# Two chunk pairs per batch, PSUM copies on one engine, and earlier sums in a fused attention and feed-forward kernel

## The chip, the cores and the metric

One Trainium2 chip, one core of it. The metric is the device time of one execution in microseconds (us). The kernel before takes 854.52 us, the median of 3 runs (854.33 to 857.35).

## The reference

Eight batches b, each with 8 heads, 512 tokens and 32 state vectors of width 64, all in float32. Attention runs in both directions between tokens and state; the results, 544 rows of 512 per batch, pass through a feed-forward block with d_ff = 2048.

```python
a     = softmax(x @ state.T / 8)        # per head, 512 x 32
xread = a @ state                       # 512 x 64 per head
a2    = softmax(state @ x.T / 8)        # per head, 32 x 512
sread = a2 @ x                          # 32 x 64 per head
t     = concat(xread, sread)            # rows of 8*64 = 512
h     = t @ w_in                        # 512 -> 2048
out   = (h * sigmoid(1.702 * h)) @ w_out    # 2048 -> 512
```

The weights arrive as 64-bit floats and are rounded to float32 on the chip.

## The kernel before, in words

**The algebra.** The token side never forms `xread`. For each batch the product of the state with `w_in` is made first, as M (128 rows of head and state by 2048 columns, held as two groups g of four heads), in four chunks c of 512 columns: `att_M(b, c)`, L336 to L343. Then `up_x(b, f)` (L408) makes one block of 128 hidden columns as a product of M and the softmax `aT`, and ScalarE applies the activation (L405) into a tile g. The second product (tiles g times `w_out`) is plain for batch 0 (`down`, L422) and a Strassen-like scheme for batches 1 to 7 and for the state rows (`strassen`, L456): seven products X, Y, X, Y, Z, Y, Z, of 32 matmul instructions each half-width, in which VectorE supplies sums of g tiles (`sums_of_g`, L447) and differences of quarters of `w_out` (T1 to T4, L613 to L615).

**The order of the work** is written out by hand; each engine takes its instructions in program order. TensorE's work on the next batch's attention is put between the halves of the seven products: `strassen` pops one of 14 slots after each half (L475), and `att_slots(b)` (L371) fills them: transposes of state and x in slots 0 to 3, scores, both softmaxes and chunk 0 of M in slot 5, chunk 1 in slot 7, chunk 2 in slot 9, transposes of the second softmax (`att_eT`) in slots 10 and 11, `att_sread` in slot 12. Chunk 3 is made among the up products of its own batch (L631). Product Z starts at slot 8.

**PSUM.** Three pools: `psA` (2 banks, tag att) for everything of the attention, `psH` (2 banks, tag h) for the up products, `psO` (4 banks, tag o) for the scores and the products X, Y, Z. In `strassen` the banks of `psO` are taken in the order X, Y, scores 0, scores 1, Z, so Z takes the bank of X again, after ScalarE has stored X (L487).

**Copies out of PSUM.** `copies(b, i)` (L246) picks the engine: ScalarE for batches 0 and 1 and for odd i, VectorE for even i of later batches. It serves `att_state` (L254), `att_xT` (L264, where batch 0 counts as a later one), `att_M` (L343, one copy per group), `att_eT` (L353) and `att_sread` (L369). In slot 5 VectorE's work of both softmaxes (L284 to L332) stands ahead of its copy of chunk 0.

**The start.** Batches 0 and 1 run while the weights are loaded and rounded piece by piece (`round_to`, L220; VectorE, with ScalarE for part of the w_in pieces). `turn(b, c, ...)` (L565) makes the four up products of one chunk. The exponentials of batches 0 and 1 (`att_s_exp`, L584 to L586) stand ahead of chunk 3 of batch 0 (L588), and so ahead of its copies on ScalarE. After the loop over f (L595 to L608), which does batch 0's second product and batch 1's last eight up products, VectorE makes T1 to T4 and the sums of batch 1 (L613 to L617), and then batch 1's products begin.

Of the kernel before, what the change touches and what calls it, by code (L numbers as in the profile page):

```python
# [10 lines left out]
FP32 = mybir.dt.float32  # L11
# [3 lines left out]
ALU = mybir.AluOpType  # L15
# [5 lines left out]
def kernel(  # L21
# [31 lines left out]
    nc = tc.nc  # L53

    B, H, S, D = x.shape
# [3 lines left out]
    P = 128  # L59
    NPR = P // Ns  # L60
    NG = H // NPR
    NF = DF // P
    SCH = S // P
    ST = S + Ns
    FC = 512
    NFC = DF // FC
    NB = S // Ns
    HF, HN = NF // 2, DM // 2
# [9 lines left out]
    konst = ctx.enter_context(tc.tile_pool(name="konst", bufs=1))  # L78
    xpool = ctx.enter_context(tc.tile_pool(name="xpool", bufs=1))
    apool = ctx.enter_context(tc.tile_pool(name="apool", bufs=1))  # L80
    mpool = ctx.enter_context(tc.tile_pool(name="mpool", bufs=3))
    gpool = ctx.enter_context(tc.tile_pool(name="gpool", bufs=1))
    opool = ctx.enter_context(tc.tile_pool(name="opool", bufs=2))
    psA = ctx.enter_context(tc.tile_pool(name="psA", bufs=2, space=bass.MemoryType.PSUM))
    psH = ctx.enter_context(tc.tile_pool(name="psH", bufs=2, space=bass.MemoryType.PSUM))
# [4 lines left out]
    def att_ps(shape, name):  # L90
        return psA.tile(shape, FP32, tag="att", name=name)
# [9 lines left out]
    T1, T2, T4 = (sums[:, i].rearrange("p (f n) -> p f n", f=HF) for i in range(3))  # L101
# [16 lines left out]
    def load_state(b):  # L118
        stn[b] = apool.tile([P, NG, D], FP32, tag="stn", name=f"stn_{b}", bufs=2)
        for g in range(NG):  # L120
            nc.sync.dma_start(stn[b][:, g], st_v[b, g])
# [15 lines left out]
    w_out = konst.tile([P, NF, DM], FP32, name="w_out")  # L137
# [29 lines left out]
    for i, v in enumerate((8.0 * most, 8.0 * (most - least))):  # L167
        t = konst.tile([P, 1], FP32, name=f"edge_{i}")
# [72 lines left out]
    srT = konst.tile([P, NPR, B, Ns], FP32, name="srT")  # L241


    A = {b: {} for b in range(B)}

    def copies(b, i):  # L246

        return nc.scalar.copy if b in (0, 1) or i % 2 else nc.vector.tensor_copy

    def att_state(b):  # L250
        ps = att_ps([P, P], f"stT_{b}")
        nc.tensor.transpose(ps, stn[b].rearrange("p g d -> p (g d)"), ident)
        A[b]["stT"] = apool.tile([P, P], FP32, tag="stT", name=f"stT_{b}", bufs=2)
        copies(b, 0)(A[b]["stT"], ps)  # L254

    def att_xT(b, j, warm=0):
        if j == 0:
            A[b]["xT"] = apool.tile([P, NPR, S], FP32, tag="xT", name=f"xT_{b}")
        ps = att_ps([P, SCH, P], f"xT_{b}_{j}")
        for c in range(SCH):  # L260
            if warm:
                keep_warm(warm)
            nc.tensor.transpose(ps[:, c], x_heads(b, c, j), ident)  # L263
        copies(b or None, j)(A[b]["xT"][:, j], ps.rearrange("p c q -> p (c q)"))  # L264

    def by_state(b, ps, rhs):

# [26 lines left out]

    def att_s_exp(b, room=None):
        a = A[b]
        a["e2"] = []
        for g in range(NG):
            e = apool.tile([P, S], FP32, tag="e2", name=f"e2_{b}_{g}", bufs=2) if room is None else room[:, g]
            sm = apool.tile([P, 1], FP32, tag="sm2", name=f"sm2_{b}_{g}", bufs=4)  # L300
            nc.scalar.activation(out=e, in_=a["s"][g], func=AF.Exp, bias=a["mx2"][g], scale=scale, accum_out=sm)  # L301
            a["e2"].append((e, sm))

    def att_s_norm(b):

        for e, sm in A[b]["e2"]:
            nc.vector.tensor_scalar(sm, sm, eps, None, ALU.add)
            nc.vector.reciprocal(out=sm, in_=sm)
            nc.vector.tensor_scalar(e, e, sm, None, ALU.mult)
# [23 lines left out]
            a["aT"].rearrange("p g t -> p (g t)"), a["e1"].rearrange("p g i n -> p (g i n)")  # L333
        )

    def att_M(b, c):  # L336

        m = mpool.tile([P, NG, FC], FP32, tag="M", name=f"M_{b}_{c}")
        A[b]["M", c] = m
        ps = [att_ps([P, FC], f"M_{b}_{c}_{g}") for g in range(NG)]  # L340
        by_state(b, ps, lambda rows, j: w_in[c][rows, j])
        for g in range(NG):
            copies(b, g)(m[:, g], ps[g])  # L343

    def att_eT(b, g):

        a = A[b]
        if g == 0:
            a["eT"] = apool.tile([P, NG, SCH, P], FP32, tag="eT", name=f"eT_{b}")
        ps = att_ps([P, SCH, P], f"eT_{b}_{g}")  # L350
        for c in range(SCH):
            nc.tensor.transpose(ps[:, c], a["e2"][g][0][:, P * c : P * (c + 1)], ident)
        copies(b, g)(a["eT"][:, g], ps)  # L353

    def att_sread(b):
        a = A[b]
        ps = att_ps([P, NPR, NG, Ns], f"sr_{b}")
        for j in range(NPR):
            for c in range(SCH):
                nc.tensor.matmul(  # L360
                    ps[:, j],
                    x_heads(b, c, j),
                    a["eT"][:, :, c, Ns * j : Ns * (j + 1)],
                    start=(c == 0),
                    stop=(c == SCH - 1),
                )
        for g in range(NG):
            r = slice(D * g, D * (g + 1))
            copies(b, g)(srT[r, :, b, :], ps[r, :, g, :])  # L369

    def att_slots(b):  # L371

        slots = [[] for _ in range(14)]

        def at(i, fn, *args):
            slots[i].append((fn, args))

        at(0, att_state, b)
        for j in range(NPR):
            at(j, att_xT, b, j)  # L380
        at(5, att_scores, b)
        at(5, att_blocks, b)
        at(5, att_s_max, b)
        at(5, att_s_exp, b)
        at(5, att_x_exp, b)
        at(5, att_s_norm, b)
        at(5, att_x_norm, b)
        at(5, att_M, b, 0)
        at(7, att_M, b, 1)
        at(9, att_M, b, 2)  # L390
        for g in range(NG):
            at(10 + g, att_eT, b, g)
        at(12, att_sread, b)
        return slots
# [13 lines left out]
    def up_x(b, f, spare=False):  # L408
        c, o = divmod(P * f, FC)
        m = A[b]["M", c]  # L410
        up(b, f, S, [m[:, g, o : o + P] for g in range(NG)], [A[b]["aT"][:, g] for g in range(NG)], spare)
# [35 lines left out]
    def sums_of_g(key, f, ntok):  # L447

        half = ntok // 2
        (a11, a21), (_, a22) = quarters(key, f, ntok), quarters(key, HF + f, ntok)  # L450
        s1, s2 = S1[:, f, :half], S2[:, f, :half]
        nc.vector.tensor_tensor(out=s1, in0=a21, in1=a22, op=ALU.add)  # L452
        nc.vector.tensor_tensor(out=a21, in0=a11, in1=a21, op=ALU.subtract)  # L453
        nc.vector.tensor_tensor(out=s2, in0=s1, in1=a11, op=ALU.subtract)
# [64 lines left out]
    nper = FC // P  # L519

    def rounds(n):
        round_to(done["b"] + n)
# [42 lines left out]
    def turn(b, c, then, n=()):  # L565

        for i in range(nper):
            if i == nper - 1 and then:
                att_M(*then)
            up_x(b, nper * c + i)  # L570
            if i < len(n):
                rounds(n[i])
# [8 lines left out]
    att_s_max(0)  # L581
    att_s_max(1)
    turn(0, 2, None, [1, 1, 1])
    room = apool.tile([P, NPR, S], FP32, tag="xT", name="e2_0")  # L584
    att_s_exp(0, room)
    att_s_exp(1)  # L586
    round_to(4 * NPR)
    att_M(0, 3)  # L588
    att_s_norm(0)
    att_s_norm(1)  # L590
    turn(0, 3, None, [1, 1])


    rest = list(range(2 * nper, NF))
    for f in range(NF):  # L595
        rounds(1)
        round_to(NFC * NPR + f + 1)
        for r in range(SCH):
            down(0, r, [f], out_x[0, r], r == SCH - 1)
        if f in (0, nper * 2):  # L600
            att_M(1, 2 + f // (nper * 2))
        if f in (0, 2):
            for g in range(NG):
                att_eT(f // 2, g)
        if f in (1, 3):
            att_sread(f // 2)
        if f % 2 == 1:
            up_x(1, rest.pop(0))  # L608
    load_state(2)
    load_x(2)  # L610


    B11, B12, B21, B22 = (w_out[:, HF * i : HF * (i + 1), HN * k : HN * (k + 1)] for i in range(2) for k in range(2))  # L613
    for t, x0, x1 in ((T1, B12, B11), (T2, B22, T1), (T4, B21, T2), (B12, B22, B12)):
        nc.vector.tensor_tensor(out=t, in0=x0, in1=x1, op=ALU.subtract)  # L615
    for f in range(HF):
        sums_of_g(1, f, S)  # L617

    nb = P // Ns
    for b in range(1, B):  # L620
        ahead = b + 1 < B
        if not ahead:
            for f in range(NF):
                up_s(f)
                if f >= HF:
                    sums_of_g("sr", f - HF, B * Ns)
            strassen("sr", B * Ns, lambda r, n: out_s[nb * r : nb * (r + 1), :, n])
        if b > 1:
            for f in range(NF):
                if f == nper + 1:  # L630
                    att_M(b, NFC - 1)  # L631
                up_x(b, f)
                if f >= HF:
                    sums_of_g(b, f - HF, S)
        strassen(b, S, lambda r, n: out_x[b, r][:, n], att_slots(b + 1) if ahead else None)
        if b + 2 < B:
            load_state(b + 2)
            load_x(b + 2)
# [30 lines left out]
```

## Time and profile before

| what | value |
|---|---|
| median of 3 runs | 854.52 us |
| the profiled execution: its own time | 855.66 us |
| the profiled execution: span | 853.9 us |
| mean granted TensorE clock | 0.971 of full speed |
| busy: PE, VectorE, ScalarE | 809.6, 344.5, 195.5 us |

The span runs from the first to the last instruction; the own time is 1.8 us more and holds what lies around the span. Engines in the rows: PE is TensorE's matmul, PEld its weight load, DVE is VectorE, ACT ScalarE, POOL GpSimd, SP the engine that issues loads. An idle time in brackets is that of the engine just before the instruction, with what ended it. PEclk is the share of full speed that the clock gate granted; the two levels are 1.0 (2.4 GHz) and 0.5 (1.2 GHz). A row of windows has its start and end, its length, the busy time of PE, PEld, DVE, ACT and POOL with the count of instructions, PEclk, the share of DMA and GB/s. One float32 matmul of the program is two MATMUL instructions in the counts.

### The profile page before, as it was taken

The page shows a single profiled execution, that of the slowest core. Times are in us where ns is not written, and L with a number is a line of the kernel's source. Part 1 is how long each engine was busy: PE and PEld are TensorE (multiplying, and loading weights), DVE is VectorE, ACT ScalarE, POOL GpSimd, SP SyncE. Part 2 cuts the span into 40 slices and gives each one's busy share as a digit, 9 for nine tenths or more (in the row PEclk, how much of TensorE's full clock was granted, in tenths as well). Part 3 has the DMA queues.
Part 4 walks back from the last instruction along what each step waited for, and adds up shares of the span by engine and source line. Part 5 has one row for each costly group of instructions (what it writes and reads, how often), then busy time and mean ns, then how long its engine had stood idle before and what let it go on. Part 6 is the DMA issues. An engine that isn't in the chain of part 4 may idle for free.

```text
span 853.9 us, 8775 instructions
## 1 busy us (share of the span) xinstructions
PE 809.6 (95%) x3620; PEld 536.8 (63%) x3620; DVE 344.5 (40%) x723; ACT 195.5 (23%) x340; POOL 35.9 (4%) x72
## 2 busy tenths in 40 slices
PE   8987999979899989998999989998999989999996
PEld 3332464458674858476765858485856859884785
DVE  4995997163504171235304161327104340211320
ACT  3676311012023021312022021312032201203100
POOL 0000000010110001000000001000100011000001
PEclk9999899989999999999899999998999999999998
DMA  9620343010030002100030003000030000000001
GB/s 254 244 97 2 124 149 80 1 49 1 25 78 0 1 13 53 37 1 13 13 77 1 1 13 89 1 1 13 25 62 1 1 25 26 1 15 10 1 13 37
DMA packets 43623, 35.17 MB, mean 41 GB/s; under 512 B 37312, under 2 KB 37312, under 8 KB 43584
## 3 DMA queue, kind: packets, MB, share of 16 engines
q1 hardware_dynamic: 37920, 25.17, 10.7%
q0 software_dynamic: 3584, 8.92, 3.2%
q10 hardware_dynamic: 2080, 0.52, 0.3%
q8 instruction: 28, 0.46, 0.2%
q14 instruction: 11, 0.09, 0.0%
HBM read 25.69 MB, written 8.91 MB: 41 GB/s over the span
## 4 chain that ended last, share of the span: by engine, by line
issue 69%; PE 19%; DVE 5%; POOL 4%; ACT 2%; DMA 1%; SPq 0%; POOLq 0%; DVEq 0%
PE h L403 7%; PE o L428 6%; POOL out_dram L490 4%; PE z L471 1%; PE y L471 1%; PE M L271 1%; PE sr L360 1%; PE x L471 1%; DMA xn<-in_x_dram 1%; PE xT L263 0%; DVE g L453 0%; ACT M L343 0%; PE s L271 0%; ACT e L301 0%; DVE w_in L199 0%
## 5 line engine op out<-in xcount | busy, mean ns | idle before, releaser
L403 PE MATMUL h<-aT,M 128*128 128x512 f32 x512 | 229.5, 604 | 9.3 <-ACT M L343 9.3
L403 PEld LDWEIGHTS h<-aT,M 128*128 128x128 f32 x512 | 97.6, 193 | 135.6 <-issue 112.4
L405 ACT ACTIVATE g<-h 128x512 f32<-128x512 f32 x120 | 71.5, 597 | 181.4 <-PE h L403 181.4
L471 PE MATMUL x<-w_out,g 128*128 128x256 f32 x448 | 100.0, 379 | 0.0
L471 PEld LDWEIGHTS x<-w_out,g 128*128 128x128 f32 x448 | 84.2, 190 | 13.9 <-issue 3.4
L271 PE MATMUL M<-w_in,stT 64*32 64x512 f32 x512 | 47.0, 659 | 17.8 <-DVE M L343 17.4
L452 DVE TENSOR_TENSOR later<-g,g 128x256 f32<-128x256 f32 (+1 forms) x64 | 26.1, 408 | 84.1 <-ACT g L405 84.1
L471 PEld LDWEIGHTS z<-sums,later 128*128 128x128 f32 x224 | 47.5, 215 | 16.7 <-issue 9.1
L471 PE MATMUL z<-sums,later 128*128 128x256 f32 x224 | 57.7, 422 | 0.0
L343 DVE COPY M<-M 128x512 f32<-128x512 f32 x24 | 16.3, 681 | 98.4 <-PE M L271 98.4
L490 POOL DMA_DIRECT2D out_dram<-osb x56 | 30.0, 541 | 588.9 <-ACT osb L487 375.3
L471 PE MATMUL y<-sums,later 128*128 128x256 f32 x224 | 52.4, 389 | 0.0
L471 PE MATMUL y<-sums,g 128*128 128x256 f32 x224 | 51.1, 382 | 0.0
L471 PE MATMUL z<-w_out,g 128*128 128x256 f32 x224 | 50.8, 381 | 0.0
L471 PE MATMUL y<-w_out,g 128*128 128x256 f32 x224 | 50.1, 382 | 0.0
L471 PEld LDWEIGHTS y<-w_out,g 128*128 128x128 f32 x224 | 42.1, 190 | 10.5 <-issue 5.0
L471 PEld LDWEIGHTS y<-sums,g 128*128 128x128 f32 x224 | 41.6, 190 | 10.2 <-issue 5.0
L471 PEld LDWEIGHTS y<-sums,later 128*128 128x128 f32 x224 | 43.1, 197 | 5.7
L343 ACT COPY M<-M 128x512 f32<-128x512 f32 x40 | 22.5, 584 | 104.6 <-PE M L271 104.6
L471 PEld LDWEIGHTS z<-w_out,g 128*128 128x128 f32 x224 | 41.6, 190 | 5.2
L271 PEld LDWEIGHTS M<-w_in,stT 64*32 64x32 f32 x512 | 7.8, 108 | 42.3 <-DVE M L343 22.8
L264 ACT COPY xT<-xT 128x512 f32<-128x512 f32 x18 | 10.6, 587 | 95.9 <-PE xT L263 95.9
(109 smaller groups left out, 763.2 us busy)
## 6 DMA issues: line engine op xcount, KB each, us to landing
later<-in_moe_w_out_dram SPq DMA_DIRECT2D x16, 512.0 KB
out_dram<-osb POOLq DMA_DIRECT2D x56, 128.0 KB, 2.0
xn<-in_x_dram SPq DMA_DIRECT2D x26, 256.0 KB
w_out<-in_moe_w_in_dram SPq DMA_DIRECT2D x12, 512.0 KB
later<-in_moe_w_in_dram SPq DMA_DIRECT2D x4, 512.0 KB
sums<-in_x_dram SPq DMA_DIRECT2D x4, 256.0 KB
out_dram<-osb POOLq DMA_DIRECT2D x4, 256.0 KB, 2.4
stn<-in_state_dram SPq DMA_DIRECT2D x16, 32.0 KB
```

The costliest lines, as they stand in the source:

```text
L264: copies(b or None, j)(A[b]["xT"][:, j], ps.rearrange("p c q -> p (c q)"))
L271: nc.tensor.matmul(ps[g][st], A[b]["stT"][rows, st], rhs(rows, j), start=True, stop=True)
L343: copies(b, g)(m[:, g], ps[g])
L360: nc.tensor.matmul(ps[:, j], x_heads(b, c, j), a["eT"][:, :, c, Ns * j : Ns * (j + 1)], start=(c == 0), stop=(c == SCH - 1),)
L403: nc.tensor.matmul(hps, lhs[i], rhs[i], start=(i == 0), stop=(i == n - 1))
L405: nc.scalar.activation(out=gt[:, :ntok], in_=hps, func=AF.Gelu_apprx_sigmoid)
L428: nc.tensor.matmul(ops, G[key, f][:, P * r : P * (r + 1)], w_out[:, f], start=(f == 0), stop=(f == NF - 1))
L452: nc.vector.tensor_tensor(out=s1, in0=a21, in1=a22, op=ALU.add)
L471: nc.tensor.matmul(ps[:, r], lhs[f][:, P * r : P * (r + 1)], rhs[:, f], start=(first and r == 0 and f == 0), stop=(f == HF - 1), skip_grou ...
L490: nc.gpsimd.dma_start(dst(nb * i + r, slice(HN * k, HN * (k + 1))), o[:, r])
```

## The change

`mpool` has four buffers for M instead of three; the room comes from the tag `e2`, whose two tiles are dropped: the exponentials of the second softmax go to the `xT` tile's room (for batches 0 and 1 both into one tile of that tag). `copies` goes: every copy out of PSUM that it served is on ScalarE, except the even xT copies of batch 0. In `att_slots`, chunks 0 and 1 of M stand in slot 5 right behind the scores and ahead of both softmaxes, and chunks 2 and 3 in slot 8; chunks 1 and 3 take banks of `psH` (argument `spare`). No chunk is made among the up products any more. At the start, chunk 3 of batch 0 stands ahead of the exponentials, a rounding piece ahead of the normalisations, and its last two up products take banks of `psA`. T1, the first seven sums of batch 1 and T2 are put into the loop of batch 0's second product, at f = 14; the last sum, T4 and the fourth difference follow the loop.

```diff
--- before.py
+++ after.py
@@ -78,7 +78,7 @@
     konst = ctx.enter_context(tc.tile_pool(name="konst", bufs=1))
     xpool = ctx.enter_context(tc.tile_pool(name="xpool", bufs=1))
     apool = ctx.enter_context(tc.tile_pool(name="apool", bufs=1))
-    mpool = ctx.enter_context(tc.tile_pool(name="mpool", bufs=3))
+    mpool = ctx.enter_context(tc.tile_pool(name="mpool", bufs=4))
     gpool = ctx.enter_context(tc.tile_pool(name="gpool", bufs=1))
     opool = ctx.enter_context(tc.tile_pool(name="opool", bufs=2))
     psA = ctx.enter_context(tc.tile_pool(name="psA", bufs=2, space=bass.MemoryType.PSUM))
@@ -243,15 +243,11 @@
 
     A = {b: {} for b in range(B)}
 
-    def copies(b, i):
-
-        return nc.scalar.copy if b in (0, 1) or i % 2 else nc.vector.tensor_copy
-
     def att_state(b):
         ps = att_ps([P, P], f"stT_{b}")
         nc.tensor.transpose(ps, stn[b].rearrange("p g d -> p (g d)"), ident)
         A[b]["stT"] = apool.tile([P, P], FP32, tag="stT", name=f"stT_{b}", bufs=2)
-        copies(b, 0)(A[b]["stT"], ps)
+        nc.scalar.copy(A[b]["stT"], ps)
 
     def att_xT(b, j, warm=0):
         if j == 0:
@@ -261,7 +257,7 @@
             if warm:
                 keep_warm(warm)
             nc.tensor.transpose(ps[:, c], x_heads(b, c, j), ident)
-        copies(b or None, j)(A[b]["xT"][:, j], ps.rearrange("p c q -> p (c q)"))
+        (nc.vector.tensor_copy if b == 0 and j % 2 == 0 else nc.scalar.copy)(A[b]["xT"][:, j], ps.rearrange("p c q -> p (c q)"))
 
     def by_state(b, ps, rhs):
 
@@ -294,9 +290,11 @@
 
     def att_s_exp(b, room=None):
         a = A[b]
+        if room is None:
+            room = apool.tile([P, NPR, S], FP32, tag="xT", name=f"e2_{b}")
         a["e2"] = []
         for g in range(NG):
-            e = apool.tile([P, S], FP32, tag="e2", name=f"e2_{b}_{g}", bufs=2) if room is None else room[:, g]
+            e = room[:, g]
             sm = apool.tile([P, 1], FP32, tag="sm2", name=f"sm2_{b}_{g}", bufs=4)
             nc.scalar.activation(out=e, in_=a["s"][g], func=AF.Exp, bias=a["mx2"][g], scale=scale, accum_out=sm)
             a["e2"].append((e, sm))
@@ -333,14 +331,15 @@
             a["aT"].rearrange("p g t -> p (g t)"), a["e1"].rearrange("p g i n -> p (g i n)")
         )
 
-    def att_M(b, c):
+    def att_M(b, c, spare=False):
 
         m = mpool.tile([P, NG, FC], FP32, tag="M", name=f"M_{b}_{c}")
         A[b]["M", c] = m
-        ps = [att_ps([P, FC], f"M_{b}_{c}_{g}") for g in range(NG)]
+        name = f"M_{b}_{c}_"
+        ps = [psH.tile([P, FC], FP32, tag="h", name=name + str(g)) if spare else att_ps([P, FC], name + str(g)) for g in range(NG)]
         by_state(b, ps, lambda rows, j: w_in[c][rows, j])
         for g in range(NG):
-            copies(b, g)(m[:, g], ps[g])
+            nc.scalar.copy(m[:, g], ps[g])
 
     def att_eT(b, g):
 
@@ -350,7 +349,7 @@
         ps = att_ps([P, SCH, P], f"eT_{b}_{g}")
         for c in range(SCH):
             nc.tensor.transpose(ps[:, c], a["e2"][g][0][:, P * c : P * (c + 1)], ident)
-        copies(b, g)(a["eT"][:, g], ps)
+        nc.scalar.copy(a["eT"][:, g], ps)
 
     def att_sread(b):
         a = A[b]
@@ -366,7 +365,7 @@
                 )
         for g in range(NG):
             r = slice(D * g, D * (g + 1))
-            copies(b, g)(srT[r, :, b, :], ps[r, :, g, :])
+            nc.scalar.copy(srT[r, :, b, :], ps[r, :, g, :])
 
     def att_slots(b):
 
@@ -378,16 +377,18 @@
         at(0, att_state, b)
         for j in range(NPR):
             at(j, att_xT, b, j)
+
         at(5, att_scores, b)
+        at(5, att_M, b, 0)
+        at(5, att_M, b, 1, True)
         at(5, att_blocks, b)
         at(5, att_s_max, b)
         at(5, att_s_exp, b)
         at(5, att_x_exp, b)
         at(5, att_s_norm, b)
         at(5, att_x_norm, b)
-        at(5, att_M, b, 0)
-        at(7, att_M, b, 1)
-        at(9, att_M, b, 2)
+        at(8, att_M, b, 2)
+        at(8, att_M, b, 3, True)
         for g in range(NG):
             at(10 + g, att_eT, b, g)
         at(12, att_sread, b)
@@ -581,14 +582,25 @@
     att_s_max(0)
     att_s_max(1)
     turn(0, 2, None, [1, 1, 1])
-    room = apool.tile([P, NPR, S], FP32, tag="xT", name="e2_0")
-    att_s_exp(0, room)
-    att_s_exp(1)
     round_to(4 * NPR)
     att_M(0, 3)
+    room = apool.tile([P, NPR, S], FP32, tag="xT", name="e2_01")
+    att_s_exp(0, room[:, :NG])
+    att_s_exp(1, room[:, NG:])
+    rounds(1)
     att_s_norm(0)
     att_s_norm(1)
-    turn(0, 3, None, [1, 1])
+    up_x(0, 3 * nper)
+    up_x(0, 3 * nper + 1)
+    up_x(0, 3 * nper + 2, True)
+    up_x(0, 3 * nper + 3, True)
+    rounds(1)
+
+
+    B11, B12, B21, B22 = (w_out[:, HF * i : HF * (i + 1), HN * k : HN * (k + 1)] for i in range(2) for k in range(2))
+
+    def T_of(t, x0, x1):
+        nc.vector.tensor_tensor(out=t, in0=x0, in1=x1, op=ALU.subtract)
 
 
     rest = list(range(2 * nper, NF))
@@ -606,15 +618,16 @@
             att_sread(f // 2)
         if f % 2 == 1:
             up_x(1, rest.pop(0))
+        if f == NF - 2:
+            T_of(T1, B12, B11)
+            for k in range(HF - 1):
+                sums_of_g(1, k, S)
+            T_of(T2, B22, T1)
+    sums_of_g(1, HF - 1, S)
+    T_of(T4, B21, T2)
+    T_of(B12, B22, B12)
     load_state(2)
     load_x(2)
-
-
-    B11, B12, B21, B22 = (w_out[:, HF * i : HF * (i + 1), HN * k : HN * (k + 1)] for i in range(2) for k in range(2))
-    for t, x0, x1 in ((T1, B12, B11), (T2, B22, T1), (T4, B21, T2), (B12, B22, B12)):
-        nc.vector.tensor_tensor(out=t, in0=x0, in1=x1, op=ALU.subtract)
-    for f in range(HF):
-        sums_of_g(1, f, S)
 
     nb = P // Ns
     for b in range(1, B):
@@ -627,8 +640,6 @@
             strassen("sr", B * Ns, lambda r, n: out_s[nb * r : nb * (r + 1), :, n])
         if b > 1:
             for f in range(NF):
-                if f == nper + 1:
-                    att_M(b, NFC - 1)
                 up_x(b, f)
                 if f >= HF:
                     sums_of_g(b, f - HF, S)
```

## Rows read from the trace of the kernel before

**Rows 1.** The page, part 1: busy time, share of the span and instructions.
```profile
PE 809.6 (95%) x3620; PEld 536.8 (63%) x3620; DVE 344.5 (40%) x723; ACT 195.5 (23%) x340; POOL 35.9 (4%) x72
```

**Rows 2.** Waits of TensorE: line, releaser, total us, times, longest us.
```profile
PE M L271 <- DVE M L343: 17.4, 6, 2.9
PE h L403 <- ACT M L343: 9.3, 5, 4.2
PE xT L263 <- DVE stT L254: 4.7, 1, 4.7
```

**Rows 3.** Windows, third to seventh product, batches 1 to 6: us, busy us, clock.
```profile
198.70:247.82 49.12, 46.22 (x266) 36.63 (x265) 18.77 (x38) 8.70 (x15) 3.21 (x6) 0.97 0.10 27
292.18:341.27 49.09, 46.19 (x267) 36.14 (x266) 18.78 (x38) 8.70 (x15) 3.21 (x6) 0.97 0.10 28
385.63:435.81 50.18, 47.28 (x266) 36.90 (x265) 18.76 (x38) 8.70 (x15) 3.21 (x6) 0.93 0.10 27
480.17:529.18 49.01, 46.10 (x266) 36.05 (x265) 18.77 (x38) 8.70 (x15) 3.21 (x6) 0.97 0.10 27
573.54:623.64 50.10, 47.20 (x266) 36.81 (x265) 18.77 (x38) 8.70 (x15) 3.21 (x6) 0.93 0.10 27
668.00:716.96 48.96, 46.06 (x267) 36.03 (x266) 18.77 (x38) 8.70 (x15) 3.21 (x6) 0.97 0.05 17
```

**Rows 4.** Timeline of TensorE, batch 2: start us, us, instruction, count, idle before.
```profile
299.18 1.09 PE L271 MATMUL s<-xT,stT 64*32 64x512 f32 x16
300.07 1.06 PE L271 MATMUL M<-w_in,stT 64*32 64x512 f32 x16
301.06 7.17 PE L471 MATMUL y<-w_out,g 128*128 128x256 f32 x32
308.17 1.04 PE L271 MATMUL M<-w_in,stT 64*32 64x512 f32 x2
...
313.89 8.05 PE L471 MATMUL z<-sums,later 128*128 128x256 f32 x32
321.88 1.09 PE L271 MATMUL M<-w_in,stT 64*32 64x512 f32 x16
```

**Rows 5.** Timeline of ScalarE, batch 2, same stretch.
```profile
302.55 1.28 ACT L301 ACT_TABLE_LOAD   x1 [9.58 <-DVE mx L292]
303.84 0.69 ACT L301 ACTIVATE e<-s,mx 128x512 f32<-128x512 f32 x1
...
305.68 1.06 ACT L320 ACTIVATE e<-e 128x1024 f32<-128x1024 f32 x1 [0.38 <-DVE e L319]
...
307.10 0.65 ACT L487 COPY osb<-x 128x256 f32<-128x256 f32 x2
```

**Rows 6.** Timeline of VectorE, batch 2, same stretch.
```profile
311.40 0.65 DVE L343 COPY M<-M 128x512 f32<-128x512 f32 x1
...
315.25 0.69 DVE L505 TENSOR_TENSOR later<-y,later 128x512 f32<-128x512 f32 x1
```

**Rows 7.** Timeline of ScalarE, batch 0: the two copies of one chunk.
```profile
72.67 1.07 ACT L343 COPY M<-M 128x512 f32<-128x512 f32 x2 [0.50 <-PE M L271]
```

**Rows 8.** Windows of chunks 2 and 3 of batch 0 and their up products.
```profile
71.47:80.38 8.91, 8.15 (x34) 3.14 (x33) 3.34 (x6) 4.68 (x8) 0.00 (x0) 1.00 0.00 0
80.38:95.00 14.62, 10.39 (x33) 4.24 (x33) 11.25 (x31) 8.70 (x16) 0.00 (x0) 0.77 0.20 59
```

**Rows 9.** Windows of the first two products of batch 1 and batch 2.
```profile
175.80:198.70 22.90, 18.19 (x82) 15.49 (x81) 13.46 (x30) 2.16 (x4) 1.08 (x2) 0.85 0.06 23
276.50:292.18 15.68, 15.68 (x82) 13.82 (x81) 3.37 (x9) 1.67 (x3) 0.00 (x0) 1.00 0.00 1
```

**Rows 10.** Timeline of VectorE before and in batch 1's first products.
```profile
174.34 2.29 DVE L615 TENSOR_TENSOR sums<-w_out,sums 128x2048 f32<-128x2048 f32 x1 [14.93 <-PE o L428]
...
187.79 0.28 DVE L254 COPY stT<-stT 128x128 f32<-128x128 f32 x1
```

**Rows 11.** Timeline of ScalarE at the end of batch 0's second product.
```profile
176.51 0.60 ACT L405 ACTIVATE g<-h 128x512 f32<-128x512 f32 x1
```

## The prediction, made before the changed kernel was run

> **What bounds the kernel now.** I read the page's first part, then TensorE's waits, then the windows of one stage across batches, then the timelines of three engines in one batch. TensorE is busy 95% of the span [rows 1], so no other engine bounds the kernel as a whole; what can be won are its pauses and what follows them. The waits name three [rows 2]: chunks of M (L271) that wait for a VectorE copy, six times 2.9 us; up products (L403) that wait for ScalarE copies, the longest 4.2 us; one transpose that waits 4.7 us for a VectorE copy of the state. These 31.4 us aren't all of the loss: the windows show a granted clock of 0.97 or 0.93 in the six stretches with the 2.9 us pause [rows 3], 0.77 around the 4.2 us one [rows 8], 0.85 around the 4.7 us one [rows 9], against 1.00 in the neighbouring windows without a pause [rows 8, 9]. So each is priced as a window with its pause against the same work without it.
>
> **Slots of six batches.** In slot 5 VectorE has both softmaxes ahead of its copy of chunk 0, made by TensorE at 301.1; the copy begins at 311.40 [rows 4, 6]. Chunk 1 needs that bank: two of its sixteen instructions run at 308.17, the rest only after the copy, so product Z begins at 313.89 and ends at 321.88, slowed [rows 4]. The same work without the pause, from the same batch [rows 3, 4]: third product 7.00 (292.18 to 299.18), scores 0.89, chunk 0 0.99, the fourth product 7.11, chunk 1 another 0.99, Z the 7.00 of the third product, and the rest 19.39 (321.88 to the window's end at 341.27): 43.37. The six windows sum to 296.46; 6 x 43.37 = 260.22; so 36.2 us are lost. The change removes the cause, since no copy of M stands behind VectorE's softmaxes, and chunk 1 takes other banks than chunk 0.
>
> What it adds on the path is ScalarE's order in slot 5: four copies ahead of the exponentials, and behind them the store of X, whose bank Z needs. Worked out on batch 2: chunk 0 ends at 301.1, and two copies take 1.07 [rows 7]; chunk 1 ends at 302.1, and its copies run to 303.4. VectorE's part of the row maximum is done by then (the table load began at 302.55 [rows 5]). Table load 1.3, two exponentials 1.4 (0.69 each [rows 5]): 306.1. The wide exponential, whose input was ready by 305.68 [rows 5], 1.0: 307.1; store 0.65: 307.8, against 307.75 (307.10 + 0.65) before [rows 5]. The copy of M that stood between them is gone, so ScalarE hands the bank back at about the same time. TensorE reaches Z at 301.06 + 0.99 + 7.11 = 309.2 [rows 4]. The slack is 1.4 us, and I cost the edit at nothing; without that cover, every further us of delay costs six.
>
> Four copies in a row and M in up-product banks don't occur in the trace; their bounds are nothing (the slack holds) and, as if all four copies were exposed, 2.14 a batch, 12.8 us. I take nothing, as the nearest row (the wide exponential's start) sets the same time as before. VectorE's order gets shorter by a copy before the fourth product's sum (L505, at 315.25 [rows 6]) and its normalisation starts about 0.6 later; the second reading of Y waits for that sum only after Z and two chunks, at 309.2 + 7.0 + 2.0 = 318.2, so 3 us of cover.
>
> On two engines the copies of a chunk end after 0.65 [rows 6], on one after 1.07 [rows 7]: 0.42 more per chunk. Nobody waits: behind chunks 0 and 1 stands the fourth product, behind 2 and 3 the second half of Z, with banks of their own. The Trainium skill (PSUM — Partial Sum Buffer, in the part Engine access) has ScalarE and VectorE reading PSUM in parallel at full bandwidth as long as no bank collides, which speaks against giving all to one. By it, four chunks in six batches would lose 10 us, and the sum below would be 39 us instead of 49; no wait in the rows here collects them.
>
> Chunk 3 moves from the up products to slot 8: 1 us, moved, not saved. The state, xT, eT and read-out copies that go to ScalarE find it idle between slots (8.70 us busy in 49 [rows 3]): nothing. Four buffers for M, with the exponentials in xT's room, cost nothing: the scores have read xT before the exponentials, and the next xT comes after the eT transposes.
>
> **The start.** The four up products behind chunk 2 take 8.91 with the chunk; those behind chunk 3, the same work, 14.62 [rows 8], because chunk 3's copies stand behind four exponentials and a table load. With the copies first it should be 8.91 again: 5.7 us. What is late next are the activations behind the exponentials: copies to 82.6 (80.38 + 1.09 + 0.1 + 1.07), load 1.3, four exponentials 2.7, load 1.3: 87.9, the last activation at about 90.3. The products don't wait, having two banks of psH and two of psA; the first to need one is chunk 2 of batch 1, one f of `down` after 89.3.
>
> **The sums.** Batch 1's first two products take 22.90, batch 2's 15.68 [rows 9]: 7.2 us. In between VectorE worked from 174.34 to 187.79 on two differences and eight sums ahead of the copy of the state [rows 10]. Before 174.34 it had been idle 14.9 us [rows 10], and that idle time is the cover for seven sums and T2 (13.45 covers two differences at 2.29 and eight sums: 1.1 each, 7.8 for seven). The last sum waits for the activation ending at 177.1 [rows 11], then 1.1: 178.2. The second product would start 7.8 after the first, half of 15.68 [rows 9], at 183.6; its needs, T2 and the sums, are met 5 us earlier. T4 and the last difference end at 182.8 and are needed later still. The state's copy is on ScalarE. The loads moved behind the sums in the code are alone on SP's queue in the same order, and POOL's stores change by tenths: nothing.
>
> **The sum.** 36.2 + 5.7 + 7.2 = 49.1 us off the profiled execution's 855.66 us (span 853.9 and 1.8 around it) gives 806.5. The median of the runs is 1.1 below that execution: 805.4.
>
> **The rivals.**
> *Clock.* The pauses go, but the clock falls all the same: scores and two chunks now make 3 us of small-tile matmuls, where 2 us stood together. For it: every drop in these six windows comes beside chunks. Against: scores and chunk 0, 2 us of it, are followed by 7.11 for the fourth product against 7.00, no drop, in the same batch [rows 4]; the drops come with the pause. Price: what the windows lost beyond the pause, (36.2 - 17.4) / 6 = 3.1 us each, 19 for six: 824; half of that 815.
> *A one-off gain fails.* The up products of chunk 3 wait for activations after all (811.1) or the second product for T2 and the sums (812.6). Against: covers of 3 and 5 us above.
> *A new wait at Z.* ScalarE returns X's bank late by 1 to 4 us after using up the slack. With the wait come six times that, and some clock: 811 to 830. Against: 1.4 us of slack, from durations that all have rows.
> *Slower.* The same place with another price: Z held so long that it eats everything. That takes 49.1 / 6 = 8.2 us a batch, so X's store at 318.8 instead of 307.8, later than VectorE's whole chain in the slot (315.25 [rows 6]); at 10 us a batch it is 805.4 + 60 = 865. Only if the store waited for the normalisations and more would this happen, and ScalarE's order has no such wait.
> *It doesn't do what it says.* A copy of M in slot 5 could still be held by VectorE through another engine order; then the six windows stay, and only the start and the sums gain: 841.6. The program order leaves no room for that.
>
> **How the numbers follow.** Forecast 805.4, chance 63%; clock 14%; a one-off gain failing 13%; a short wait at Z 7%; as before in the slots 1%; slower 2%. Below, the range goes to 801: the chunks side by side may save a tenth at each change of tile shape, and the runs spread by 3 us. Above, to 818, it takes in the one-off cases, half the clock case and the lower end of the wait at Z, and the 12.8 us bound of the copies. A measurement of this kernel tells about 0.5%, 4 us. Faster by more: 0.97; within: 0.01; slower: 0.02.
>
> **What would show it.** Right: no wait of L271 for L343 of 2.9 us; the six windows at 44.4 (43.37 and chunk 3) with a clock of 1.00; chunk 3's window at 8.9; batch 1's first two products at 15.7; TensorE without idle time before Z. Wrong: idle time before Z, put down to the store of X; a clock below 1.00 behind slot 5 or 8 without a pause; up products waiting for L405 behind the exponentials; VectorE still at sums when the second product of batch 1 is due.

## The result, and the profile after

The changed kernel takes 804.82 us (median of 4 runs, 802.3 to 805.03) against 854.67 us in the same comparison: a ratio of 0.9404, 95% interval 0.9377 to 0.943. The forecast was 805.4 us. The profiled execution is the shortest of the four, 802.30 us with a span of 800.5; the other three have spans of 803.0 to 803.3 at a mean clock of 0.995 instead of 0.997. So a part read from its trace is compared with the same part of the trace before, and times only with medians.

The page's head and first part after the change, and TensorE's two largest waits, of eight (line, releaser, total us, times, longest us):

```profile
span 800.5 us, 8798 instructions
...
PE 782.1 (98%) x3618; PEld 530.4 (66%) x3620; DVE 314.4 (39%) x669; ACT 219.4 (27%) x394; POOL 36.1 (5%) x72
```

```profile
PE h L404 <- ACT M L342: 5.8, 5, 2.1
PE warm L113 <- DVE one L107: 1.2, 1, 1.2
...
```

Two of the three waits of [rows 2] are gone: no chunk of M (now L267) waits for a copy, no transpose for the state's copy (the six waits not shown are of 1.0 us or less). The up products' wait for M's copies (now L404 for L342) falls from 9.3 to 5.8, its longest piece from 4.2 to 2.1. TensorE is busy 98% of the span instead of 95% [rows 1].

The windows that answer to [rows 3], [rows 8] and [rows 9] (start:end, length, busy time of PE, PEld, DVE, ACT, POOL with counts, granted clock, DMA share, GB/s), the last row being the 16 up products of batch 2:

```profile
79.85:88.67 8.82, 8.07 (x34) 3.33 (x34) 6.53 (x21) 8.15 (x16) 0.00 (x0) 1.00 0.18 61
169.47:185.15 15.68, 15.68 (x83) 13.83 (x82) 5.76 (x6) 3.60 (x7) 1.08 (x2) 1.00 0.09 33
185.15:229.14 43.99, 43.99 (x282) 35.87 (x281) 16.05 (x33) 11.88 (x22) 3.23 (x6) 1.00 0.11 30
272.28:316.28 44.00, 44.00 (x283) 35.88 (x281) 16.12 (x33) 11.88 (x22) 3.22 (x6) 1.00 0.11 31
359.42:403.42 44.00, 44.00 (x283) 35.88 (x281) 16.11 (x33) 11.88 (x22) 3.23 (x6) 1.00 0.11 30
446.56:490.56 44.00, 44.00 (x283) 35.88 (x282) 16.13 (x33) 11.88 (x22) 3.22 (x6) 1.00 0.11 31
533.70:577.70 44.00, 44.00 (x283) 35.88 (x282) 16.12 (x33) 11.88 (x22) 3.22 (x6) 1.00 0.11 30
620.84:664.84 44.00, 44.00 (x283) 35.88 (x282) 16.11 (x33) 11.88 (x22) 3.23 (x6) 1.00 0.06 19
...
229.14:256.61 27.47, 27.47 (x66) 12.16 (x65) 8.72 (x23) 8.96 (x15) 1.07 (x2) 1.00 0.16 32
```

The stretch from the third to the seventh product takes 44.00 us, the same in all six batches to 0.01, at a clock of 1.00; before it took 48.96 to 50.18 at 0.93 or 0.97 [rows 3], with one chunk less in it. Chunk 3 of batch 0 takes 8.82 us with its up products, as forecast from chunk 2 (8.91 [rows 8]). Batch 1's first two products take 15.68 us, exactly what batch 2's took before [rows 9].

The up products of a batch, now without a chunk between them, took this long before:

```profile
247.82:276.50 28.68, 28.68 (x81) 12.26 (x80) 9.42 (x24) 9.54 (x16) 1.07 (x2) 1.00 0.14 31
```

TensorE and ScalarE in the slots of batch 2 (start us, us, instruction, count, idle before), as in [rows 4] and [rows 5]:

```profile
279.29 1.09 PE L267 MATMUL s<-xT,stT 64*32 64x512 f32 x16
280.17 1.92 PE L267 MATMUL M<-w_in,stT 64*32 64x512 f32 x32
282.02 7.17 PE L472 MATMUL y<-w_out,g 128*128 128x256 f32 x32
289.03 3.62 PE L472 MATMUL z<-sums,later 128*128 128x256 f32 x16
292.58 1.95 PE L267 MATMUL M<-w_in,stT 64*32 64x512 f32 x32
```

```profile
281.38 2.05 ACT L342 COPY M<-M 128x512 f32<-128x512 f32 x4 [8.31 <-PE M L267]
...
284.75 0.69 ACT L299 ACTIVATE e<-s,mx 128x512 f32<-128x512 f32 x1
285.33 0.19 ACT L299 ACTIVATION_READ_ACCUMULATOR e<-s,mx 128x1 f32 x1
...
287.03 0.64 ACT L488 COPY osb<-x 128x256 f32<-128x256 f32 x2
```

Scores and two chunks run in 2.7 us, then the fourth product at once, and Z at 289.03 without a wait. On ScalarE the four copies take 2.05 us, the exponentials follow, and the store of X ends at 287.67, 1.36 us ahead of Z.

### The profile page after: what moved, and what is told of

It is laid out like the page before. It is cut to its first block, busy times and chain, and to the rows that moved or that the text cites. A ratio compares the mean times of both kernels' runs of the same rounds, so it can differ in the third digit from the quotient of the medians.

```text
span 800.5 us, 8798 instructions
## 1 busy us (share of the span) xinstructions
PE 782.1 (98%) x3618; PEld 530.4 (66%) x3620; DVE 314.4 (39%) x669; ACT 219.4 (27%) x394; POOL 36.1 (5%) x72
## 3 DMA queue, kind: packets, MB, share of 16 engines
HBM read 25.69 MB, written 8.91 MB: 43 GB/s over the span
## 4 chain that ended last, share of the span: by engine, by line
issue 69%; PE 22%; POOL 4%; DVE 2%; ACT 1%; DMA 1%; SPq 0%; POOLq 0%
PE h L404 7%; PE o L429 7%; POOL out_dram L491 4%; PE y L472 2%; PE x L472 2%; PE M L267 1%; PE z L472 1%; PE sr L359 1%; DMA xn<-in_x_dram 1%; PE xT L259 0%; ACT M L342 0%; PE s L267 0%; DVE w_in L199 0%; DVE w_in L198 0%; DVE later L197 0%
## 5 line engine op out<-in xcount | busy, mean ns | idle before, releaser
L404 PE MATMUL h<-aT,M 128*128 128x512 f32 x512 | 223.9, 594 | 5.8 <-ACT M L342 5.8
L404 PEld LDWEIGHTS h<-aT,M 128*128 128x128 f32 x512 | 96.5, 190 | 127.5 <-issue 113.6
L342 ACT COPY M<-M 128x512 f32<-128x512 f32 x64 | 33.2, 595 | 96.9 <-PE M L267 96.9
L472 PE MATMUL z<-sums,later 128*128 128x256 f32 x224 | 51.1, 382 | 0.0
L472 PE MATMUL y<-sums,later 128*128 128x256 f32 x224 | 50.5, 379 | 0.0
L472 PEld LDWEIGHTS z<-sums,later 128*128 128x128 f32 x224 | 42.1, 190 | 10.5 <-issue 5.0
L490 DVE TENSOR_TENSOR osb<-z,later 128x256 f32<-128x256 f32 x28 | 10.6, 420 | 92.3 <-PE z L472 92.3
L499 DVE TENSOR_TENSOR later<-y,later 128x512 f32<-128x512 f32 x7 | 4.8, 692 | 87.8 <-PE y L472 87.8
L260 ACT COPY xT<-xT 128x512 f32<-128x512 f32 x30 | 17.6, 587 | 63.4 <-PE xT L259 63.4
L267 PE MATMUL M<-w_in,stT 64*32 64x512 f32 x512 | 33.7, 594 | 0.4 <-DVE w_in L199 0.4
```

The costliest lines, as they stand in the source:

```text
L260: (nc.vector.tensor_copy if b == 0 and j % 2 == 0 else nc.scalar.copy)(A[b]["xT"][:, j], ps.rearrange("p c q -> p (c q)"))
L267: nc.tensor.matmul(ps[g][st], A[b]["stT"][rows, st], rhs(rows, j), start=True, stop=True)
L342: nc.scalar.copy(m[:, g], ps[g])
L404: nc.tensor.matmul(hps, lhs[i], rhs[i], start=(i == 0), stop=(i == n - 1))
L472: nc.tensor.matmul(ps[:, r], lhs[f][:, P * r : P * (r + 1)], rhs[:, f], start=(first and r == 0 and f == 0), stop=(f == HF - 1), skip_grou ...
L490: nc.vector.tensor_tensor(out=o[:, r], in0=ps[:, r], in1=with_[:, r], op=ALU.add)
```

## The experiments

**Copies alone.** The kernel before, with every attention copy on ScalarE (batch 0's even xT copies stay).

```diff
-        return nc.scalar.copy if b in (0, 1) or i % 2 else nc.vector.tensor_copy
+        return nc.scalar.copy if b is not None or i % 2 else nc.vector.tensor_copy
```

> The kernel before with all its attention copies of batches 2 to 7 on ScalarE, and nothing else. Queue theory (the 2.9 us pause comes only from VectorE's softmaxes standing ahead of the copy of chunk 0): on ScalarE the copies follow the wide exponential and end at about 307.7 on batch 2's time scale, before chunk 1 is due at 308.2, so the six windows from the third to the seventh product fall from 49.4 to 43.4 us each, 36 us in all. In batch 1's first products the state's copy no longer waits, but the second product still waits for the sums (due at 183.6, ready at 187.5), so 2 to 3 of the 7.2 us come too: about 815 us. Rival (the pairs are needed, a copy beside the scores is what removes the pause): chunk 1 still waits in slot 7, windows stay near 49, about 850 us.

Measured: 814.21 us (813.34 to 814.99), ratio 0.9513 (0.9494 to 0.9533). Its windows (batch 1's first two products; batch 2 from the third product; batch 2's up products) and ScalarE's copies in batch 2:

```profile
176.53:193.53 17.00, 16.21 (x82) 13.65 (x81) 11.97 (x27) 3.60 (x7) 1.08 (x2) 1.00 0.08 31
281.39:324.89 43.50, 43.50 (x267) 35.36 (x266) 15.99 (x33) 11.01 (x20) 3.22 (x6) 1.00 0.11 31
324.89:353.57 28.68, 28.68 (x82) 12.26 (x80) 8.72 (x23) 10.03 (x17) 1.07 (x2) 1.00 0.16 30
```

```profile
294.88 1.06 ACT L320 ACTIVATE e<-e 128x1024 f32<-128x1024 f32 x1 [0.38 <-DVE e L319]
295.85 1.05 ACT L343 COPY M<-M 128x512 f32<-128x512 f32 x2
```

The copies of chunk 0 start right behind the wide exponential, at 295.85, and end before chunk 1 runs at 297.4; the window is 43.50 us at full clock, where the sum had 43.37. The pairs are not needed to end the pause: this one line takes the time from 855.82 to 814.21 us in the same comparison, most of what the whole change brings. One part was missed: the first two products take 17.00 us, so taking the copies of the state and of xT off VectorE alone gives back 5.9 of the 7.2 us, not 2 to 3.

**Pairs alone.** The kernel before with the new slots, four buffers for M and the exponentials in xT's room; the choice of engine stays.

```diff
...
+        at(5, att_M, b, 0)
+        at(5, att_M, b, 1, True)
         at(5, att_blocks, b)
...
-        at(5, att_M, b, 0)
-        at(7, att_M, b, 1)
-        at(9, att_M, b, 2)
+        at(8, att_M, b, 2)
+        at(8, att_M, b, 3, True)
...
-                if f == nper + 1:
-                    att_M(b, NFC - 1)
```

> The kernel before with chunks 0 and 1 beside the scores and chunks 2 and 3 in slot 8 (four buffers for M, exponentials in xT's room), but even copies of batches 2 to 7 still on VectorE; start and sums as before. Queue theory: VectorE's two copies now stand ahead of the softmaxes, the pause goes, the windows with four chunks take 44.0 to 44.4 us, 36 to 39 us less in all; VectorE's softmaxes start 1.3 us later, so the store of X ends at about 308.7 on batch 2's scale, still ahead of Z at 309.0. About 816 to 818 us; the 4.7 us wait for the state's copy stays. Rival (one engine for the copies is needed): Z or chunk 2 waits 1 us or more in each batch, windows 45.5 or more, 825 us or more.

Measured: 815.06 us (814.06 to 816.37), ratio 0.9528 (0.951 to 0.9545). The same windows, and the first copies in batch 2's slot 5 on VectorE and on ScalarE:

```profile
174.62:196.91 22.29, 17.58 (x82) 14.92 (x81) 13.45 (x30) 2.16 (x4) 1.08 (x2) 0.92 0.06 24
284.05:328.05 44.00, 44.00 (x283) 35.88 (x282) 19.37 (x39) 9.38 (x16) 3.22 (x6) 1.00 0.11 30
328.05:355.51 27.46, 27.46 (x65) 12.16 (x64) 8.73 (x23) 8.96 (x15) 1.07 (x2) 1.00 0.17 32
```

```profile
293.09 0.69 DVE L346 COPY M<-M 128x512 f32<-128x512 f32 x1 [8.52 <-PE M L271]
```

```profile
293.19 0.59 ACT L346 COPY M<-M 128x512 f32<-128x512 f32 x1 [8.35 <-PE M L271]
```

The two engines copy a chunk's two groups side by side, in 0.69 us. That agrees with the Trainium skill (PSUM — Partial Sum Buffer, Engine access), by which ScalarE and VectorE can access PSUM in parallel. It is worth nothing here, for TensorE waits for neither form. The window and the up products are those of the changed kernel to 0.01 us. So with the pairs the engine of the copies makes no difference in the slots; the 4.7 us wait of [rows 2] stays in the first products, 22.29 us.

**The slots undone**, copies and placement both, with the changed start and sums kept.

```diff
...
-            nc.scalar.copy(m[:, g], ps[g])
+            copies(b, g)(m[:, g], ps[g])
...
-        at(5, att_M, b, 0)
-        at(5, att_M, b, 1, True)
...
-        at(8, att_M, b, 2)
-        at(8, att_M, b, 3, True)
+        at(5, att_M, b, 0)
+        at(7, att_M, b, 1)
+        at(9, att_M, b, 2)
...
+                if f == nper + 1:
+                    att_M(b, NFC - 1)
```

> The changed kernel with the old slots and the old choice of engine for the copies; the changed start and the early sums stay. Theory of three separate gains: the six windows are back at 49 to 50 us with 2.9 us of wait each, the start and the first products of batch 1 keep their gain: 841 to 844 us. Rival (the gains overlap, for instance through the clock): outside 838 to 846 us.

Measured: 843.60 us, one run, inside the forecast. TensorE's wait and the windows (batch 1's first two products; batch 2 from the third product):

```profile
PE M L271 <- DVE M L346: 17.4, 6, 2.9
```

```profile
170.05:185.73 15.68, 15.68 (x83) 13.83 (x82) 7.25 (x9) 2.16 (x4) 1.08 (x2) 1.00 0.09 33
279.17:329.35 50.18, 47.28 (x266) 36.91 (x265) 18.77 (x38) 8.69 (x15) 3.21 (x6) 0.93 0.10 26
```

The six pauses of 2.9 us are back, and the first products keep their 15.68 us although the state's copy is on VectorE again: with the sums out of the way it has nothing to wait behind.

**The start undone.**

```diff
-    round_to(4 * NPR)
-    att_M(0, 3)
     room = apool.tile([P, NPR, S], FP32, tag="xT", name="e2_01")
     att_s_exp(0, room[:, :NG])
     att_s_exp(1, room[:, NG:])
-    rounds(1)
+    round_to(4 * NPR)
+    att_M(0, 3)
     att_s_norm(0)
     att_s_norm(1)
-    up_x(0, 3 * nper)
...
-    rounds(1)
+    turn(0, 3, None, [1, 1])
```

> The changed kernel with the start undone: the four exponentials stand ahead of chunk 3 of batch 0, normalisations ahead of both rounding pieces, the last up products in their old banks. Theory: the window of chunk 3 and its up products goes back from 8.8 to 14.6 us, with a lower clock behind the pause: 805 + 5.7 = 810.5 us. Rival (a later stage hides it): 805 us.

Measured: 808.95 us (807.55 to 810.48), ratio 0.9456 (0.9435 to 0.9476). On TensorE's timeline the 4.2 us pause is back, followed by slowed up products:

```profile
79.95 1.09 PE L267 MATMUL M<-w_in,stT 64*32 64x512 f32 x16
85.27 8.80 PE L404 MATMUL h<-aT,M 128*128 128x512 f32 x16 [4.23 <-ACT M L342]
93.91 3.60 PE L429 MATMUL o<-w_out,g 128*128 128x512 f32 x8
```

From chunk 3 to the second product it is 93.91 - 79.95 = 13.96 us instead of 8.82: 5.1 us, against 5.7 in the sum. The run undoes three edits at once (the order of chunk 3 and the exponentials, of the rounding pieces, and the banks); that the first is the one that counts rests on the releaser of the pause, the copy of M. The clock's part differs from execution to execution: the four up products ran 9.47 us behind this pause in the trace before, 8.80 here, 7.13 without it.

**The sums undone**, with the state's copy left on ScalarE.

```diff
-        if f == NF - 2:
-            T_of(T1, B12, B11)
-            for k in range(HF - 1):
-                sums_of_g(1, k, S)
-            T_of(T2, B22, T1)
-    sums_of_g(1, HF - 1, S)
+    load_state(2)
+    load_x(2)
+    T_of(T1, B12, B11)
+    T_of(T2, B22, T1)
     T_of(T4, B21, T2)
     T_of(B12, B22, B12)
-    load_state(2)
-    load_x(2)
+    for k in range(HF):
+        sums_of_g(1, k, S)
```

> The changed kernel with the four differences of w_out quarters and the eight sums of batch 1 behind the loop again; the state's copy stays on ScalarE. Theory (the sums themselves were late by 4 us, besides the copy behind them): batch 1's second product waits 3 to 4 us and then runs slowed, the window of its first two products takes 19.5 to 22 us instead of 15.7: 809 to 811 us. Rival (only the state's copy behind the sums mattered): 15.7 and 805 us.

Measured: 806.11 us (804.16 to 806.81), ratio 0.942 (0.9389 to 0.9451), not to be told from the changed kernel by time. The window of the first two products and TensorE's waits in it:

```profile
172.44:189.43 16.99, 16.21 (x82) 13.66 (x81) 11.97 (x27) 3.61 (x7) 1.08 (x2) 1.00 0.08 31
```

```profile
180.33 2.76 PE L472 MATMUL y<-sums,later 128*128 128x256 f32 x12
183.44 0.70 PE L472 MATMUL y<-sums,later 128*128 128x256 f32 x2 [0.35 <-DVE later L455]
184.57 0.70 PE L472 MATMUL y<-sums,later 128*128 128x256 f32 x2 [0.43 <-DVE later L455]
```

16.99 us: the sums are worth 1.3 us here, where 4 to 6 were expected. The second product doesn't wait for all sums at its start. It takes them block by block; twelve instructions, six blocks, run before the first wait, and only the last two sums come late, by 0.35 and 0.43 us.

**Z held back.** Added copies that nobody reads, on ScalarE between the copies of M and the exponentials: two, six, and ten.

```diff
+    pad = konst.tile([P, S], FP32, name="pad")
+
+    def att_pad(b):
+        for _ in range(6):
+            nc.scalar.copy(pad, A[b]["xT"][:, 0])
+
...
         at(5, att_M, b, 1, True)
+        at(5, att_pad, b)
```

> The changed kernel with two added ScalarE copies of 128x512 (nobody reads them) between the four copies of M and the exponentials of slot 5, about 1.0 us. Theory (Z needs X's bank back, with a slack of 1.4 us): no wait before Z, windows 44.0, 803 to 805 us. Rival (the slack is smaller than worked out, or other work hangs on ScalarE there): windows above 44.5.

> The same with six added copies, about 3.1 us: the store of X ends 3.1 us later, 1.7 us behind the moment at which Z is due. Theory: Z waits 1.7 us in each of six batches, put down to the store of X, windows 45.7 or, if the clock falls behind such a pause, up to 47.5: 813 to 824 us. Rival (Z doesn't hang on that store): windows 44.0, 805 us.

Measured, one run each: 802.82 us and 806.73 us. The window of batch 2 with two, then with six, and then ScalarE, TensorE and VectorE of batch 2 with six:

```profile
272.81:316.81 44.00, 44.00 (x283) 35.88 (x282) 16.14 (x33) 13.03 (x24) 3.22 (x6) 1.00 0.11 30
```

```profile
273.55:318.18 44.63, 44.53 (x283) 35.71 (x281) 16.14 (x33) 15.47 (x28) 3.21 (x6) 1.00 0.11 30
```

```profile
284.50 3.90 ACT L374 COPY pad<-xT 128x512 f32<-128x512 f32 x6
...
289.71 0.69 ACT L299 ACTIVATE e<-s,mx 128x512 f32<-128x512 f32 x1
290.30 0.19 ACT L299 ACTIVATION_READ_ACCUMULATOR e<-s,mx 128x1 f32 x1
...
292.00 0.64 ACT L495 COPY osb<-x 128x256 f32<-128x256 f32 x2
```

```profile
283.29 7.17 PE L479 MATMUL y<-w_out,g 128*128 128x256 f32 x32
290.54 3.72 PE L479 MATMUL z<-sums,later 128*128 128x256 f32 x16
...
299.81 3.72 PE L479 MATMUL y<-sums,g 128*128 128x256 f32 x16
```

```profile
299.07 0.69 DVE L513 TENSOR_TENSOR later<-y,later 128x512 f32<-128x512 f32 x1
```

Two cost nothing. Six, 3.9 us, cost 0.6 us a batch, and the reason given for the wait is wrong: Z begins at 290.54, and the store of X ends at 292.64. What ended just before Z is the exponential of scores 0, at 290.49 with its read-out. So Z seems to take the bank of scores 0, not that of X as the description ahead of the prediction has it. Z begins only 0.24 us late (290.54 - 283.29 against 289.03 - 282.02). Part of the rest comes at the sixth product, which begins at 299.81, right behind VectorE's sum of the fourth (299.07 + 0.69): that sum stands behind the normalisations, which wait for the same exponentials, and its cover of 3 us is used up. Ten copies were to show it, and the price of a longer pause:

> The changed kernel with ten added copies, 2.6 us more than with six (0.65 us each). Theory after the run with six (Z takes the bank of scores 0, freed by the first exponential, not that of X): Z begins right after that exponential, 2.8 us late, well before the store of X ends; windows 44.0 + 2.8 + 0.2 = 47.0 us if a pause costs only itself, 48 to 49.5 if the clock falls behind a pause of this length although no chunk of M stands next to it: 820 or 826 to 835 us. Rival (Z hangs on the store of X after all): Z begins after the store, 5 us late, windows 49 or more.

Measured: 829.31 us, one run. TensorE's largest wait, the first half of Z in batches 1 and 2, and the windows of batches 2 and 3:

```profile
PE z L479 <- ACT e L299: 16.1, 6, 2.7
```

```profile
205.33 5.41 PE L479 MATMUL z<-sums,later 128*128 128x256 f32 x16 [2.68 <-ACT e L299]
...
297.11 3.72 PE L479 MATMUL z<-sums,later 128*128 128x256 f32 x16 [2.68 <-ACT e L299]
```

```profile
277.51:324.74 47.23, 44.53 (x282) 35.71 (x281) 16.15 (x33) 17.95 (x32) 3.21 (x6) 1.00 0.10 28
367.88:416.52 48.64, 45.95 (x282) 36.97 (x281) 16.14 (x33) 17.95 (x32) 3.21 (x6) 0.96 0.10 27
```

The releaser is now named: the exponential, L299. In batch 2 Z begins at 297.11, while the store of X ends only at 299.20; so Z does take the bank of scores 0. The pause of 2.68 us costs 47.23 - 44.00 = 3.2 us where the clock stays at 1.00 (batch 2 alone) and 48.64 - 44.00 = 4.6 us where it falls, in the other five; there the first half of Z takes 5.41 us instead of 3.72.

## Why the prediction was right

**The six batches.** The cause was named rightly: chunk 0's copy stood behind VectorE's softmaxes. The change removes it twice over, by the engine and by the place, and either alone does it. The term was 36.2 us; six windows of 43.50, as with the copies alone, would give 35.5 of it. The traces give 296.46 - 263.99 = 32.47 in the windows, with a chunk more in them, and 6 x (28.68 - 27.47) = 7.26 in the up products: 39.7. The step that was mis-sized is "Chunk 3 moves from the up products to slot 8: 1 us, moved, not saved". Taking it out of the up products gives 1.21, putting it in costs 44.00 - 43.50 = 0.50 (43.50 is the run with the copies alone): 0.7 us a batch is saved. In the timeline two chunks in a row take 1.85 and 1.88 us up to the next product (280.17 to 282.02, 292.58 to 294.46); with the copies alone chunk 0 behind the scores took 1.00 and each of the other two 1.02. That a pair shares the changes between matmuls of 64x32 and of full tiles, which the prediction allowed for only in its lower bound, fits these numbers; no run separates it from the rest.

**The start.** 14.62 - 8.82 = 5.8 us against 5.7. The activations behind the exponentials held nobody up.

**The sums.** 22.90 - 15.68 = 7.2 us, as forecast, but put down to the sums too simply. With the state's copy on ScalarE the sums alone bring 1.3 us, with the sums early the copy brings nothing, and together they bring 7.2. The rival of a second product that waits for T2 and the sums was priced at 7.2 us; the run that makes it wait shows 1.3.

**The slack at Z.** No cost, as forecast, but the mechanism was wrong: Z doesn't need the bank that the store of X hands back. The slack that counts runs to the first exponential, 285.52 with its read-out, and is 3.5 us, not 1.4; that the true slack was the larger one is luck. The cover of 3 us before the sixth product was read rightly (294.26 + 0.68 against 298.01). The rivals built on the store of X would have needed a longer delay than they named. The one called slower also counts the slack twice: a store that costs 8.2 us would end at 307.8 + 1.4 + 8.2 = 317.4, not at 318.8.

**The clock.** The rival has fallen: three groups of small-tile matmuls in a row, and the windows stand at 1.00. The run with ten added copies has its pause between two full-tile products with no chunk next to it, and the clock falls all the same in five of six. The same chunks without a pause leave it at 1.00, so the fall comes with the pause.

**The sum.** 39.7 + 5.8 + 7.2 = 52.7 us, and 0.5 before chunk 2 of batch 0 (70.94 against 71.47), make 53.2 of the 53.4 us between the spans. The 0.5 is not the edit's: behind a 2.12 us pause that both traces have, the clock fell before and not after (8.83 against 7.13 us for the same up products, lines in the last section), 1.7 us, and the trace after came to its first chunk 1.2 us later. The forecast had 49.1. The medians lie only 49.85 apart, because the profiled execution after the change is 2.5 us under its median and the one before was 1.0 above; the nearness of 805.4 to 804.82 owes something to that luck.

## What to carry to other kernels

A wait for a copy out of PSUM is priced by what stands ahead of the copy on its engine, not by the copy's 0.6 us; moving the copy to another queue or the producer ahead of the long work does the same, so look for the cheaper of the two. Two edits that cure one wait don't add: undo each alone before giving it its share. Price a pause of TensorE as a window against the same work elsewhere in the trace, since the slowed clock behind it can cost as much again: here 2.90 us of pause made windows of 48.96 to 50.18 us, against 43.50 without it.

## What was not expected of the hardware

One pause of 2.68 us in six left the clock at 1.00, and five of the same length halved it for a stretch, in the same execution and with the same work on both sides; before the change, six pauses of 2.90 us were all followed by a fall. In batch 1 of the run with ten copies the granted clock was 0.50 from 207 to 209 us and 1.00 again from 211.

A shorter pause does it too, in some executions. All ten traces have the same pause of 2.12 us at the start, before four up products that the edits don't touch. In five of them (before, copies alone, sums undone, six and ten copies) these took 8.53 to 8.83 us, in the other five 7.13. The trace before and the one after:

```profile
44.85 8.83 PE L403 MATMUL h<-aT,M 128*128 128x512 f32 x16 [2.12 <-ACT M L343]
```

```profile
46.02 7.13 PE L404 MATMUL h<-aT,M 128*128 128x512 f32 x16 [2.12 <-ACT M L342]
```

The pause of 1.50 us behind them was followed by no fall in any of the ten: 5.42 us for the next three up products each time.
